# One decode step with gradients on one core: the zero fill reads bf16 instead of u8, the row tiles share one buffer, and the weight gradients are staged in two regions instead of six

## The chip, the core and the metric

The kernel runs on one core of a Trainium2 chip. The number that counts is the device time of one execution in microseconds. The median of three runs of the kernel before is 820.67 us (818.9 to 821.32).

A core has five engines that run side by side: PE (TensorE, matrix products), DVE (VectorE), ACT (ScalarE), POOL (GpSimd) and SP (SyncE). Here SP only issues transfers. Each engine works through its own instructions in order and waits on semaphores for the others. Sixteen DMA engines move data between the main memory of the chip (HBM) and the on-chip buffer (SBUF, 128 partitions). Transfers issued by SP are in one queue, those issued by POOL in another, and both are served by the same sixteen engines.

## The reference

One decode step of a transformer block, forward and backward, for a batch of B = 2, one token, width D = 512.

```python
def _A_ref(x, k_cache, v_cache, wq, wo):      # attention over the last W = 4096 of 32768 cached rows
    q = (x @ wq).reshape(B, Sq, 32, 128).transpose(0, 2, 1, 3)
    k = jnp.repeat(k_cache[:, :, Sk - W:, :], 4, axis=1)      # 8 cached heads, 32 query heads
    v = jnp.repeat(v_cache[:, :, Sk - W:, :], 4, axis=1)
    p = _softmax(jnp.einsum("bhqd,bhkd->bhqk", q, k) * (128 ** -0.5), axis=-1)
    o = jnp.einsum("bhqk,bhkd->bhqd", p, v)
    return o.transpose(0, 2, 1, 3).reshape(B, Sq, 4096) @ wo

def _B_ref(x, w_gate, w_up, w_down):          # F = 1792
    return (_gelu(x @ w_gate) * (x @ w_up)) @ w_down

h = A_x + _A_ref(_layernorm(A_x), A_k_cache, A_v_cache, A_wq, A_wo)
h2 = h + _B_ref(_layernorm(h), B_w_gate, B_w_up, B_w_down)
```

The outputs are `h2` and the gradients, for a given `grad_out`, of A_x, the K cache, the V cache, A_wq, A_wo, B_w_gate, B_w_up and B_w_down, all in bf16. The gradients of the two caches have the caches' own shape (2 x 8 x 32768 x 128): they are zero in all rows but the last 4096 of each head. Those zeros are 224 MiB (32 pieces of 7 MiB) and by far the largest part of what is written.

## The kernel before

**The zero fill.** A tile `zt` of 128 x 1024 zeros is made on DVE by masking a part of w_q with 0 (L118), so it waits for w_q's load. Then POOL issues 32 transfers (`zero_cast`, L104), one for each zero region. Each reads rows of `zt` again and again and casts them to f32 on the way; the bf16 output is seen as f32 for this, so one row of 1024 elements becomes 4 KiB of zeros. In the kernel before `zt` is u8, so a row is 1 KiB at its source. POOL holds eight of these transfers in flight, and issues the next when one has completed.

**The memory.** Nearly all of SBUF is one tile `mem` of 198 KiB in each partition, cut by hand: `at(off, ...)` gives a view at a byte offset, and the tables at the head of the file (`K_OFF`, `PK_OFF`, `OFF_GST`, `OFF_ST` and so on) say which region serves which purpose and when. Order and waits follow from overlaps of these regions; a scheduler in the programming layer puts the instructions of each engine in order when the program is built. Evictions from PSUM to SBUF (`evac`, L88 on DVE and L90 on ACT) take turns between the two engines.

**The stages**, in order of time:

- `attention(0)` and `attention(1)`, one for each batch entry. K and V come head by head through SP (L125, L129). PE turns K (L332), takes the scores (L342), DVE and ACT make the product of K and the exponentials (`pk`, L374 and L377), and PE sums it with V (L382, L388). At batch 1 a later head's K or V goes into a region that an earlier head has left. `pk` of batch 1 is two regions of 4 KiB at 180 and 184 KiB.
- `middle(0)` and `middle(1)`: output projection (L460, L468), second layernorm, feed-forward part and the backward pass down to the gradient of the attention's output. At the end of attention, SP loads w_down again (L137), since K and `pk` have overwritten it, and at batch 1 a copy of the input rows x (L112), which had been overwritten too. L460 is the first matmul of `attn_ps`; it adds x from a tile at partitions 32 and 33 (`x_32`). That tile and `grad_out` (`dh2_bf`, at partitions 0 and 1) are in `dh2_x`, loaded once at the start by ACT (L116, L117) into a pool of their own.
- `score_grads(0)` and `score_grads(1)`: V is turned (L596, copied by L88 and L90) and multiplied by the output's gradient (L605). During `score_grads(1)` the gradients of w_o, w_down, w_gate and w_up are made as well, two units after each step: a unit is one matmul (L665), an eviction into a staging region and, at the end of its group, a store. There are six groups, in this order: 14, 14 and 4 blocks of w_o's gradient (L675), 14 of w_down's (L693), 16 pieces for w_gate and 16 for w_up (L700). Each group has a staging region of its own (`OFF_GST`, L57).
- The gradient of w_q and of x: L225 turns w_q's blocks, L745 makes four blocks of w_q's gradient, each staged in its own 8 KiB of w_q's region and stored by L748. DVE's L726 reads x again here.
- The tail: the last 4096 rows of the caches' gradients. L774 makes them, L88 and L90 evict them into regions of 16 KiB, taken in turn from `OFF_ST` (eight of them), and L782 stores them, 32 transfers of 1 MiB.

Of the kernel before, what the change touches and what calls it, by code (L numbers as in the profile page):

```python
# [16 lines left out]
P = 128  # L17
B, D = 2, 512
HQ, HKV, REP, DH = 32, 8, 4, 128
# [4 lines left out]
NBH = B * HQ  # L24
F = 1792
NFR = F // P
NDR = D // P
# [17 lines left out]
OFF_DS = (196 * KIB, OFF_M)  # L45
MEM_BYTES = 198 * KIB
OFF_R0, OFF_R1, OFF_R2 = OFF_R, OFF_R + 2 * KIB, OFF_R + 4 * KIB
OFF_LN2B, OFF_DHB, OFF_X = OFF_R + 6 * KIB, OFF_R + 7 * KIB, OFF_R + 8 * KIB

K_OFF = ([OFF_WG + (g % 4) * 8 * KIB for g in range(HKV)],  # L50
         [OFF_WD, OFF_WD + 8 * KIB, 32 * KIB, 40 * KIB, 48 * KIB, 56 * KIB, OFF_WD, OFF_WD + 8 * KIB])
# [2 lines left out]
          [OFF_WD + 16 * KIB + i * 4 * KIB for i in range(2)])  # L54

OFF_BD = OFF_WO
OFF_GST = [OFF_WG, OFF_WG + 14 * KIB, OFF_WO, OFF_WO + 14 * KIB, 0, 16 * KIB]  # L57
OFF_FROW = OFF_WD
OFF_DH = OFF_WD + 4 * KIB
OFF_L = OFF_WD + 5 * KIB  # L60
OFF_RO = OFF_WD + 6 * KIB
OFF_ST = [OFF_WG, OFF_WG + 16 * KIB] + [i * 16 * KIB for i in range(4)] + [OFF_WQ, OFF_WQ + 16 * KIB]

@with_exitstack
def kernel(ctx, tc, A_x, A_k_cache, A_v_cache, A_wq, A_wo, B_x, B_w_gate, B_w_up, B_w_down, grad_out,
                out_0, out_1, out_2, out_3, out_4, out_5, out_6, out_7, out_8):
    nc = tc.nc
# [5 lines left out]
    rows = ctx.enter_context(tc.tile_pool(name="rows", bufs=1))  # L73
# [22 lines left out]
    dVv = out_3[:, :, Z:, :].rearrange("b g (p j) d -> p b g j d", p=P)  # L96

    ZE = 1024
    zt = const.tile([P, ZE], U8)
    zero_regions = [o[b, g, 0:Z, :].rearrange("r d -> (r d)") for o in (out_2, out_3) for b in range(B) for g in range(HKV)]  # L100

    def zero_cast(i):
# [1 line left out]
        nc.gpsimd.dma_start(out=zero_regions[i].bitcast(F32).rearrange("(p k e) -> p k e", p=P, k=nper),  # L104
                            in_=zt[:].unsqueeze(1).to_broadcast([P, nper, ZE]))

    dh2_x = rows.tile([34, D], BF16)
    dh2_bf, x_32 = dh2_x[0:B, :], dh2_x[32:32 + B, :]
    x_bf = at(OFF_X, [B, D], BF16, "x")

    def load_x():
        nc.sync.dma_start(out=x_bf[:], in_=A_x.rearrange("b s d -> (b s) d"))  # L112
    load_x()
    wq_sb = at(OFF_WQ, [P, NDR, HQ * DH], BF16, "wq")
    nc.sync.dma_start(out=wq_sb[:], in_=A_wq.rearrange("(p r) n -> p r n", r=NDR))
    nc.scalar.dma_start(out=dh2_bf, in_=grad_out.rearrange("b s d -> (b s) d"))  # L116
    nc.scalar.dma_start(out=x_32, in_=A_x.rearrange("b s d -> (b s) d"))  # L117
    nc.vector.tensor_scalar(out=zt[:].bitcast(U32), in0=wq_sb[:, 0, 0:ZE // 2].bitcast(U32), scalar1=0, scalar2=None,  # L118
                            op0=ALU.bitwise_and)

    Kt, Vt = {}, {}
# [17 lines left out]
    def load_wg_wu():  # L139
# [31 lines left out]
    for base in (0, -HQ):  # L171
        nc.gpsimd.affine_select(out=maskC[:], in_=maskC[:], compare_op=ALU.not_equal, fill=1.0,
                                base=base, pattern=[[-1, HQ]], channel_multiplier=1)
    selB = const.tile([B, NBH], BF16)
    nc.gpsimd.memset(selB[:], 1.0)
    nc.gpsimd.affine_select(out=selB[:], in_=selB[:], compare_op=ALU.is_ge, fill=0.0,
                            base=0, pattern=[[1, NBH]], channel_multiplier=-HQ)
    nc.gpsimd.affine_select(out=selB[:], in_=selB[:], compare_op=ALU.is_ge, fill=0.0,
                            base=HQ - 1, pattern=[[-1, NBH]], channel_multiplier=HQ)
    for i in range(len(zero_regions)):  # L180
        zero_cast(i)

# [10 lines left out]
        nc.vector.tensor_copy(out=y_bf[:], in_=y[:])  # L193
        return mv, rstd

    def transpose_rows(ps, src_bf, name, strided):
        for r in range(NDR):
            src = src_bf[:, r::NDR] if strided else src_bf[:, r * P:(r + 1) * P]
            nc.tensor.transpose(out=ps[:, r, :], in_=src, identity=ident_bf[:B, :B])
# [73 lines left out]
    def prefetch(b, g):  # L273
        if b == 0:
            if g == 0:
                for i in range(4):
                    load_k(0, i)
                    load_v(0, i)
                for i in range(4, HKV):
                    load_v(0, i)  # L280
            elif g + 3 < HKV:
                load_k(0, g + 3)
            if g == 1:
                nc.sync.dma_start(out=wo_sb[:], in_=A_wo.rearrange("(p r) n -> p r n", r=NOR))
        else:
            if g == 0:
                for i in range(4):
                    load_k(1, i)
                    load_v(1, i)
                load_k(1, 4)  # L290
                load_k(1, 5)
            elif g in (1, 2):
                load_k(1, g + 5)
            elif g - 3 + 4 < HKV:
                load_v(1, g + 1)
        if g == HKV:
            if b == 0:
                load_wg_wu()
            load_wd()
            if b == 1:  # L300
                load_x()

    def attention(b):
        with tc.tile_pool(name="ps_KT", bufs=2, space=PSUM) as ps_KT, \
# [135 lines left out]
            nc.vector.tensor_scalar(out=p_bf[b][:], in0=ps[:].rearrange("p a k -> p (a k)"), scalar1=rl[:, 0:1], scalar2=None, op0=ALU.mult)  # L440

    ln2_bf = at(OFF_LN2B, [B, D], BF16, "ln2b")
    dh_bf = at(OFF_DHB, [B, D], BF16, "dhb")
    O2 = small.tile([P, NOR, B], BF16)
    nc.vector.memset(O2[:], 0.0)
    dact = small.tile([P, NFR * B], F32)
# [6 lines left out]
    dh = at(OFF_R2, [B, D], F32, "dh")  # L453

    def middle(b):
        h0 = b * HQ
        with tc.tile_pool(name="ps_W", bufs=2, space=PSUM) as ps_W, \
# [88 lines left out]
            nc.vector.tensor_copy(out=dh_bf[:], in_=dh[:])  # L546
            dhT = transpose_rows(ps_B.tile([P, NDR, B], BF16, tag="sm", name="psT_dh"), dh_bf[:], f"dh{b}", strided=False)

            dO2_ps = ps_B.tile([P, NOR, B], F32, tag="da", name="dO2_ps")

# [70 lines left out]
    score_grads(0)  # L621
    attention(1)
    middle(1)

    o_bhd = small.tile([NBH, DH], BF16, tag="bhd")
    DH_bf = at(OFF_DH, [NBH, D], BF16, "DH")
# [9 lines left out]
    with tc.tile_pool(name="ps_G", bufs=2, space=PSUM) as ps_G:  # L636
# [5 lines left out]
        nc.tensor.matmul(out=DH_ps[:], lhsT=selB[:], rhs=dh_bf[:], start=True, stop=True)  # L642
# [4 lines left out]
        GST = 14 * D  # L647
# [3 lines left out]
        def add_group(n_cols_list, lhsT_fn, rhs_fn, store_fn):  # L651
            st_box = {}
            offs = [0]
            for n in n_cols_list:
                offs.append(offs[-1] + n)

            def unit(k):
                def f():
                    if k == 0:
                        st_box["st"] = at(OFF_GST[gst_i[0]], [P, GST], BF16, "gst")  # L660
                        gst_i[0] += 1
                    st = st_box["st"]
# [48 lines left out]
    with tc.tile_pool(name="ps_W2", bufs=2, space=PSUM) as ps_W, \  # L711
# [19 lines left out]
        nc.vector.tensor_copy(out=dh_bf[:], in_=dx[:])  # L731
        nc.sync.dma_start(out=out_1.rearrange("b s d -> (b s) d"), in_=dh_bf[:])

        L_ps = ps_Q.tile([NBH, D], F32, tag="x")
        nc.tensor.matmul(out=L_ps[:], lhsT=selB[:], rhs=ln2_bf[:], start=True, stop=True)
        L_bf = at(OFF_L, [NBH, D], BF16, "L")
        nc.vector.tensor_copy(out=L_bf[:], in_=L_ps[:])
        gwq_v = out_4.rearrange("(p r) n -> p r n", r=NDR)
        for r in range(NDR):
            st = at(OFF_WQ + r * 8 * KIB, [P, HQ * DH], BF16, "gq")  # L740
            for c4 in range(4):
                ps = ps_G.tile([P, 1024], F32, tag="ps_g", name="ps_gq")
                for q in range(2):
                    col0 = c4 * 1024 + q * 512
                    nc.tensor.matmul(out=ps[:, q * 512:(q + 1) * 512], lhsT=L_bf[:, r::NDR],  # L745
                                     rhs=Ro_flat[:, col0:col0 + 512], start=True, stop=True)
                evac(st[:, c4 * 1024:(c4 + 1) * 1024], ps[:])
            nc.sync.dma_start(out=gwq_v[:, r, :], in_=st[:])  # L748
# [63 lines left out]
```

## Time and profile before

| | |
|---|---|
| median of three runs | 820.67 us |
| the profiled execution | 820.67 us, span 819.0 us |
| mean granted TensorE clock | 0.817 |
| PE, DVE, ACT, POOL busy | 595.0, 510.1, 443.7, 35.9 us |
| DMA | 332.48 MB in 69462 packets, mean 406 GB/s |
| POOL's queue (q0, the zero fill) | 57856 packets, 234.88 MB |
| SP's queue (q1) | 11532 packets, 96.74 MB |
| `prefetch`, L137 at batch 1 | issued at 477.19 us |
| stores of the six weight-gradient groups | issued at 579.4, 590.3, 593.4, 617.9, 640.4 and 657.4 us |
| first store of the tail (L782) | issued at 712.0 us |

The span runs from the first to the last instruction of the profiled execution; the time is that of the whole execution. A line of a timeline has the start and the duration in us, the engine, the line of the kernel, the operation, output and inputs, shapes and count, and in square brackets how long the engine had been idle before and what released it. A line of the DMA view has a queue's packets, its megabytes and the time of its packets as a share of what sixteen engines have in the window; it can be over 100%, since the packets of an engine overlap. "DMA to landing" is the time from a transfer's issue to its semaphore.

### The profile page before, as it was taken

The numbers are of one execution on the slowest core, as the hardware profiler recorded it, in microseconds if no ns is written. First come the engines' busy times: TensorE is split into PE (matmuls) and PEld (weight loads), VectorE is DVE, ScalarE is ACT, GpSimd is POOL, SyncE is SP. The second block draws the span as 40 slices with busy tenths as digits, with TensorE's granted clock in tenths as the row PEclk, the third lists the DMA queues.
The fourth block names the chain that finished last, engine by engine and source line by source line (L and its number), as shares of the span: only waits on it lengthen the run. The fifth ranks groups of instructions, "written<-read, shape, count | busy, mean of one in ns | idle before, by whom it ended". The sixth has DMA issues, their size and how long they took to land.

```text
span 819.0 us, 13345 instructions
## 1 busy us (share of the span) xinstructions
PE 595.0 (73%) x5350; PEld 324.3 (40%) x5350; DVE 510.1 (62%) x893; ACT 443.7 (54%) x1016; POOL 35.9 (4%) x49
## 2 busy tenths in 40 slices
PE   3787877808978845878574786977988697777782
PEld 3454443307566533444242334564433242222220
DVE  2899789703243323979485762435656637999993
ACT  1898889403333423979383742332645434576683
POOL 4100000001000000000000000000000000000000
PEclk9999999965866985989697895955956587888897
DMA  8999999999999999999999999999999999976968
GB/s 363 415 422 418 420 422 422 428 420 424 422 423 422 417 416 425 423 421 419 424 425 422 423 429 418 424 423 423 427 416 423 426 424 425 363 296 281 389 274 343
DMA packets 69462, 332.48 MB, mean 406 GB/s; under 512 B 1804, under 2 KB 1816, under 8 KB 59288
## 3 DMA queue, kind: packets, MB, share of 16 engines
q0 software_dynamic: 57856, 234.88, 86.2%
q1 hardware_dynamic: 11532, 96.74, 49.7%
q8 instruction: 42, 0.69, 0.3%
q10 hardware_dynamic: 12, 0.01, 0.2%
q14 instruction: 20, 0.16, 0.1%
HBM read 49.29 MB, written 282.33 MB: 405 GB/s over the span
## 4 chain that ended last, share of the span: by engine, by line
PE 26%; DVE 13%; DMA 11%; ACT 5%; issue 2%; ACTq 0%; DVEq 0%; SPq 0%
DMA mem<-in_A_v_cache_dram 7%; DVE mem L88 5%; ACT mem L90 4%; PE ps_g L774 4%; PE ps_gr L665 4%; PE ps_tb L225 4%; DMA mem<-in_B_w_down_dram 4%; DVE mem L374 3%; PE M_ps L388 3%; PE VT_ps L596 3%; PE dP_ps L605 2%; DVE mem L685 2%; DVE mem L253 2%; PE ps_gq L745 1%; PE d_ln_ps L722 1%
## 5 line engine op out<-in xcount | busy, mean ns | idle before, releaser
L374 DVE TENSOR_TENSOR mem<-mem,ef 128x1024 bf16<-128x1024 bf16 (+1 forms) x256 | 213.7, 875 | 19.0 <-PE M_ps L388 18.9
L377 ACT ACTIVATE mem<-mem,ef 128x128 bf16<-128x128 bf16 x640 | 200.5, 391 | 24.0 <-PE M_ps L388 21.4
L388 PE MATMUL M_ps<-mem 128*128 128x512 bf16 x512 | 142.4, 399 | 36.5 <-DVE mem L374 31.4
L90 ACT COPY mem<-ps_tb 128x512 bf16<-128x512 bf16 x83 | 48.5, 585 | 126.1 <-PE ps_tb L225 74.4
L225 PE MATMUL ps_tb<-ident_bf,mem 128*128 128x128 bf16 x664 | 82.0, 267 | 26.7 <-DMA mem<-in_B_w_down_dram 18.5
L774 PE MATMUL ps_g<-mem 128*128 128x512 bf16 x256 | 81.8, 421 | 24.4 <-ACT mem L90 20.2
L88 DVE COPY mem<-ps_tb 128x512 bf16<-128x512 bf16 x83 | 35.2, 424 | 95.2 <-PE ps_tb L225 63.6
L90 ACT CAST mem<-ps_g 128x512 bf16<-128x512 f32 x128 | 74.7, 585 | 31.9 <-DVE mem L88 27.2
L88 DVE CAST mem<-ps_g 128x512 bf16<-128x512 f32 x128 | 83.2, 687 | 7.4 <-PE ps_g L774 6.6
L388 PEld LDWEIGHTS <-mem 128*128 128x128 bf16 x512 | 42.9, 100 | 98.5 <-DVE mem L374 55.0
L225 PEld LDWEIGHTS <-mem 128*128 128x128 bf16 x664 | 55.5, 129 | 53.3 <-issue 29.7
L332 PE MATMUL KT_ps<-ident_bf,mem 128*128 128x128 bf16 x512 | 46.5, 242 | 31.4 <-DMA mem<-in_A_k_cache_dram 21.3
L90 ACT COPY mem<-KT_ps 128x1024 bf16<-128x1024 bf16 x32 | 32.1, 1002 | 58.4 <-PE KT_ps L332 58.4
L774 PEld LDWEIGHTS <-mem 128*128 128x128 bf16 x256 | 26.6, 104 | 78.8 <-issue 64.9
L104 POOL DMA_DIRECT2D out_dram<-zt x32 | 33.7, 1142 | 517.4 <-DMA out_dram<-zt 506.2
L332 PEld LDWEIGHTS <-mem 128*128 128x128 bf16 x512 | 36.3, 109 | 43.3 <-DMA mem<-in_A_k_cache_dram 21.9
L90 ACT COPY mem<-VT_ps 128x1024 bf16<-128x1024 bf16 x33 | 34.0, 1031 | 33.9 <-PE VT_ps L596 25.6
L605 PE MATMUL dP_ps<-mem 128*128 128x512 bf16 x128 | 45.1, 437 | 4.5 <-ACT mem L90 4.5
L596 PE MATMUL VT_ps<-ident_bf,mem 128*128 128x128 bf16 x512 | 46.5, 242 | 0.9 <-DVE pkT L572 0.9
L596 PEld LDWEIGHTS <-mem 128*128 128x128 bf16 x512 | 37.4, 109 | 24.7 <-issue 17.2
L88 DVE CAST mem<-ps_gr 128x512 bf16<-128x512 f32 (+1 forms) x40 | 26.7, 671 | 28.9 <-PE ps_gr L665 28.8
L382 PE MATMUL oPK_ps<-mem 128*4 128x128 bf16 x512 | 28.8, 235 | 21.5 <-DMA mem<-in_A_v_cache_dram 21.5
(253 smaller groups left out, 626.6 us busy)
## 6 DMA issues: line engine op xcount, KB each, us to landing
out_dram<-zt POOLq DMA_DIRECT2D x32, 7168.0 KB, 163.2
out_dram<-mem SPq DMA_DIRECT2D x36, 1024.0 KB, 10.4
mem<-in_A_k_cache_dram SPq DMA_DIRECT2D x16, 1024.0 KB, 17.4
mem<-in_A_v_cache_dram SPq DMA_DIRECT2D x16, 1024.0 KB, 29.8
out_dram<-mem SPq DMA_DIRECT2D x5, 1792.0 KB, 24.1
mem<-in_A_wq_dram SPq DMA_DIRECT2D x1, 4096.0 KB, 12.2
mem<-in_A_wo_dram SPq DMA_DIRECT2D x1, 4096.0 KB
mem<-in_B_w_down_dram SPq DMA_DIRECT2D x2, 1792.0 KB, 27.3
```

The lines of the kernel that those rows point to most:

```text
L88: nc.vector.tensor_copy(out=out, in_=in_)
L90: nc.scalar.copy(out=out, in_=in_)
L104: nc.gpsimd.dma_start(out=zero_regions[i].bitcast(F32).rearrange("(p k e) -> p k e", p=P, k=nper), in_=zt[:].unsqueeze(1).to_broadcast([P, ...
L225: nc.tensor.transpose(out=ps[:, a, :], in_=src_block(a), identity=ident_bf[:])
L332: nc.tensor.transpose(out=KT_ps[:, jj, :], in_=Kt[b, g][:, u * 8 + jj, :], identity=ident_bf[:])
L374: nc.vector.tensor_tensor(out=pk[:, 0:n, h0:h1, :], in0=Kb[:, j0:j0 + n, :].unsqueeze(2).to_broadcast(shape), in1=ef[:, j0:j0 + n, h0:h1]. ...
L377: nc.scalar.activation(out=pk[:, jj, i, :], in_=Kb[:, j0 + jj, :], func=ACT.Copy, scale=ef[:, j0 + jj, i:i + 1])
L388: nc.tensor.matmul(out=M_ps[:], lhsT=Vt[b, g][:, j, :], rhs=pk[:, jj, :, :].rearrange("p i d -> p (i d)"), start=(j == 0), stop=(j == NJ - 1))
L596: nc.tensor.transpose(out=VT_ps[:, jj, :], in_=Vt[b, g][:, a * 8 + jj, :], identity=ident_bf[:])
L605: nc.tensor.matmul(out=dP_ps[:, c, :], lhsT=dOpad[:, w0:w0 + P], rhs=VT[:, c * 4:(c + 1) * 4, :].rearrange("d a k -> d (a k)"), start=(i = ...
L665: nc.tensor.matmul(out=ps[:, :n], lhsT=lhsT_fn(k), rhs=rhs_fn(k), start=True, stop=True)
L774: nc.tensor.matmul(out=ps[:, a2, :], lhsT=lhs_bf[:, jp * P:(jp + 1) * P], rhs=rhs_bd[:, ap * 2 + a2, gq * 4:(gq + 1) * 4, :].rearrange("q ...
```

## The change

Three things change together.

- `zt` becomes bf16 (2 KiB in each partition instead of 1), so that the zero fill casts bf16 to f32. The fill's rows are 2 KiB at the source, and still 4 KiB at the destination.
- The pool of the row tile goes. `dh2_x` becomes a view of `mem` at 185 KiB with 66 partitions: `grad_out` at 0 and 1, x at 32 and 33, and `dh_bf` (the gradient rows, until now a region of their own) at 64 and 65. Since `pk` of batch 1 passes over these bytes, `load_rows` loads `grad_out` and x a second time at the end of `attention(1)`, through SP, after w_down. The other copy of x is now loaded after `middle(1)`, in a part of the region that M has left. A matmul that reads `dh_bf` takes its other operand from partitions 64 and 65 too, so `selB` has a copy there.
- The six groups of weight gradients use two regions of 14 KiB in turn, and so do the four blocks of w_q's gradient after them. A region is written again when its store has landed. The tail has six regions instead of eight, and begins with the ones that V has left.

```diff
-OFF_LN2B, OFF_DHB, OFF_X = OFF_R + 6 * KIB, OFF_R + 7 * KIB, OFF_R + 8 * KIB
+OFF_LN2B, OFF_XR = OFF_R + 6 * KIB, OFF_R + 7 * KIB
+OFF_X, OFF_X_AGAIN = OFF_LN2B, OFF_M + 2 * KIB
...
-OFF_GST = [OFF_WG, OFF_WG + 14 * KIB, OFF_WO, OFF_WO + 14 * KIB, 0, 16 * KIB]
+OFF_GST = OFF_WG
...
-OFF_ST = [OFF_WG, OFF_WG + 16 * KIB] + [i * 16 * KIB for i in range(4)] + [OFF_WQ, OFF_WQ + 16 * KIB]
+OFF_ST = [i * 16 * KIB for i in range(4)] + [OFF_WG, OFF_WG + 16 * KIB]
...
-    zt = const.tile([P, ZE], U8)
+    zt = const.tile([P, ZE], BF16)
...
-    dh2_x = rows.tile([34, D], BF16)
-    dh2_bf, x_32 = dh2_x[0:B, :], dh2_x[32:32 + B, :]
-    x_bf = at(OFF_X, [B, D], BF16, "x")
...
+    dh2_x = at(OFF_XR, [66, D], BF16, "xr")
+    dh2_bf, x_32, dh_bf = dh2_x[0:B, :], dh2_x[32:32 + B, :], dh2_x[64:64 + B, :]
+
+    def load_rows(eng):
+        eng.dma_start(out=dh2_bf, in_=grad_out.rearrange("b s d -> (b s) d"))
+        eng.dma_start(out=x_32, in_=A_x.rearrange("b s d -> (b s) d"))
+
+    def load_x(off):
+        x_bf = at(off, [B, D], BF16, "x")
         nc.sync.dma_start(out=x_bf[:], in_=A_x.rearrange("b s d -> (b s) d"))
-    load_x()
+        return x_bf
+    x_bf = load_x(OFF_X)
...
-    nc.scalar.dma_start(out=dh2_bf, in_=grad_out.rearrange("b s d -> (b s) d"))
-    nc.scalar.dma_start(out=x_32, in_=A_x.rearrange("b s d -> (b s) d"))
-    nc.vector.tensor_scalar(out=zt[:].bitcast(U32), in0=wq_sb[:, 0, 0:ZE // 2].bitcast(U32), scalar1=0, scalar2=None,
+    load_rows(nc.scalar)
+    nc.vector.tensor_scalar(out=zt[:].bitcast(U32), in0=wq_sb[:, 0, 0:ZE].bitcast(U32), scalar1=0, scalar2=None,
                             op0=ALU.bitwise_and)
...
-    selB = const.tile([B, NBH], BF16)
+    selB_all = const.tile([66, NBH], BF16)
...
             if b == 1:
-                load_x()
+                load_rows(nc.sync)
...
-    dh_bf = at(OFF_DHB, [B, D], BF16, "dhb")
...
     middle(1)
+    x_bf = load_x(OFF_X_AGAIN)
...
-                        st_box["st"] = at(OFF_GST[gst_i[0]], [P, GST], BF16, "gst")
+                        st_box["st"] = at(OFF_GST + (gst_i[0] % 2) * 14 * KIB, [P, GST], BF16, "gst")
...
-            st = at(OFF_WQ + r * 8 * KIB, [P, HQ * DH], BF16, "gq")
+            st = at(OFF_GST + (r % 2) * 14 * KIB, [P, HQ * DH], BF16, "gq")
```

More of the change, by code (lines that the diff above doesn't have):

```diff
@@ L72 @@
     small = ctx.enter_context(tc.tile_pool(name="small", bufs=1))
-    rows = ctx.enter_context(tc.tile_pool(name="rows", bufs=1))
     mem_pool = ctx.enter_context(tc.tile_pool(name="mem", bufs=1))
@@ L105, in zero_cast @@
                             in_=zt[:].unsqueeze(1).to_broadcast([P, nper, ZE]))
-    dh2_x = rows.tile([34, D], BF16)
-    dh2_bf, x_32 = dh2_x[0:B, :], dh2_x[32:32 + B, :]
-    x_bf = at(OFF_X, [B, D], BF16, "x")
-    def load_x():
+    dh2_x = at(OFF_XR, [66, D], BF16, "xr")
[5 more added lines that the diff above has]
+        x_bf = at(off, [B, D], BF16, "x")
         nc.sync.dma_start(out=x_bf[:], in_=A_x.rearrange("b s d -> (b s) d"))
-    load_x()
+        return x_bf
+    x_bf = load_x(OFF_X)
     wq_sb = at(OFF_WQ, [P, NDR, HQ * DH], BF16, "wq")
     nc.sync.dma_start(out=wq_sb[:], in_=A_wq.rearrange("(p r) n -> p r n", r=NDR))
-    nc.scalar.dma_start(out=dh2_bf, in_=grad_out.rearrange("b s d -> (b s) d"))
-    nc.scalar.dma_start(out=x_32, in_=A_x.rearrange("b s d -> (b s) d"))
-    nc.vector.tensor_scalar(out=zt[:].bitcast(U32), in0=wq_sb[:, 0, 0:ZE // 2].bitcast(U32), scalar1=0, scalar2=None,
+    load_rows(nc.scalar)
+    nc.vector.tensor_scalar(out=zt[:].bitcast(U32), in0=wq_sb[:, 0, 0:ZE].bitcast(U32), scalar1=0, scalar2=None,
                             op0=ALU.bitwise_and)
@@ L173 @@
                                 base=base, pattern=[[-1, HQ]], channel_multiplier=1)
-    selB = const.tile([B, NBH], BF16)
[L175 to L179, printed above, removed]
+    selB_all = const.tile([66, NBH], BF16)
+    nc.gpsimd.memset(selB_all[:], 1.0)
+    selB, selB_64 = selB_all[0:B, :], selB_all[64:64 + B, :]
+    for sel in (selB, selB_64):
+        nc.gpsimd.affine_select(out=sel, in_=sel, compare_op=ALU.is_ge, fill=0.0,
+                                base=0, pattern=[[1, NBH]], channel_multiplier=-HQ)
+        nc.gpsimd.affine_select(out=sel, in_=sel, compare_op=ALU.is_ge, fill=0.0,
+                                base=HQ - 1, pattern=[[-1, NBH]], channel_multiplier=HQ)
     for i in range(len(zero_regions)):
@@ L194, in layernorm, with transpose_rows @@
         return mv, rstd
-    def transpose_rows(ps, src_bf, name, strided):
+    def transpose_rows(ps, src_bf, name, strided, p0=0):
         for r in range(NDR):
             src = src_bf[:, r::NDR] if strided else src_bf[:, r * P:(r + 1) * P]
-            nc.tensor.transpose(out=ps[:, r, :], in_=src, identity=ident_bf[:B, :B])
+            nc.tensor.transpose(out=ps[:, r, :], in_=src, identity=ident_bf[p0:p0 + B, p0:p0 + B])
         dst = small.tile([P, NDR, B], BF16, name=f"T_{name}", tag=f"T_{name[:-1]}")
@@ L545, in middle @@
             ln_bwd(d_ln2_ps[:].rearrange("b a p -> b p a"), ln2[:], rstd2, dh2_bf, f"2{b}", dh, at(OFF_R0, [B, D], F32, "tmp"))
-            nc.vector.tensor_copy(out=dh_bf[:], in_=dh[:])
-            dhT = transpose_rows(ps_B.tile([P, NDR, B], BF16, tag="sm", name="psT_dh"), dh_bf[:], f"dh{b}", strided=False)
+            nc.vector.tensor_copy(out=dh_bf, in_=dh[:])
+            dhT = transpose_rows(ps_B.tile([P, NDR, B], BF16, tag="sm", name="psT_dh"), dh_bf, f"dh{b}", strided=False, p0=64)
             dO2_ps = ps_B.tile([P, NOR, B], F32, tag="da", name="dO2_ps")
@@ L641 @@
         DH_ps = ps_G.tile([NBH, D], F32, tag="g", name="DH_ps")
-        nc.tensor.matmul(out=DH_ps[:], lhsT=selB[:], rhs=dh_bf[:], start=True, stop=True)
+        nc.tensor.matmul(out=DH_ps[:], lhsT=selB_64, rhs=dh_bf, start=True, stop=True)
         nc.vector.tensor_copy(out=DH_bf[:], in_=DH_ps[:])
@@ L730 @@
         ln_bwd(d_ln1_ps[:].rearrange("b a p -> b p a"), ln1[:], rstd1, dh[:], "1", dx, at(OFF_FROW + 2 * KIB, [B, D], F32, "tmp"))
-        nc.vector.tensor_copy(out=dh_bf[:], in_=dx[:])
-        nc.sync.dma_start(out=out_1.rearrange("b s d -> (b s) d"), in_=dh_bf[:])
+        nc.vector.tensor_copy(out=dh_bf, in_=dx[:])
+        nc.sync.dma_start(out=out_1.rearrange("b s d -> (b s) d"), in_=dh_bf)
         L_ps = ps_Q.tile([NBH, D], F32, tag="x")
-        nc.tensor.matmul(out=L_ps[:], lhsT=selB[:], rhs=ln2_bf[:], start=True, stop=True)
+        nc.tensor.matmul(out=L_ps[:], lhsT=selB, rhs=ln2_bf[:], start=True, stop=True)
         L_bf = at(OFF_L, [NBH, D], BF16, "L")
```

## The prediction

> **What bounds the kernel now.** The page's slices come first: the row of the DMA engines is full from the second slice on, at about 424 GB/s, until slice 34 (700 us); after that no engine group is full and the last stage (L774 and its evictions) runs on PE, DVE and ACT.
>
> ```profile
> DMA  8999999999999999999999999999999999976968
> HBM read 49.29 MB, written 282.33 MB: 405 GB/s over the span
> out_dram<-zt POOLq DMA_DIRECT2D x32, 7168.0 KB, 163.2
> ```
>
> The zero fill keeps the engines full, and it does not bound the time by itself: 332.48 MB at 424 GB/s are 784 us of the 819. The time goes to compute that waits for small transfers behind the fill. PE's timeline, read for idle time that a DMA ended (last bracket), shows it:
>
> ```profile
> 184.15 1.04 PE L225 MATMUL ps_tb<-ident_bf,mem 128*128 128x128 bf16 x8 [18.47 <-DMA mem<-in_B_w_down_dram]
> 316.92 0.72 PE L332 MATMUL KT_ps<-ident_bf,mem 128*128 128x128 bf16 x5 [16.55 <-DMA mem<-in_A_k_cache_dram]
> 400.56 0.29 PE L382 MATMUL oPK_ps<-mem 128*4 128x128 bf16 x4 [9.96 <-DMA mem<-in_A_v_cache_dram]
> 447.85 0.29 PE L382 MATMUL oPK_ps<-mem 128*4 128x128 bf16 x4 [9.60 <-DMA mem<-in_A_v_cache_dram]
> 506.57 1.44 PE L541 MATMUL ffn_ps<-mem,actT_bf 128*2 128x512 bf16 x3 [4.83 <-DMA mem<-in_B_w_down_dram]
> ```
>
> With 2.58 at 82 us and 1.94 at 467 us this is 64 us. SP's timeline and the chain of waits give one such transfer whole: 1.8 MB of w_down, issued at 477.19, release PE 29.4 us later.
>
> ```profile
> 477.19 0.33 SPq L137 DMA_DIRECT2D mem<-in_B_w_down_dram  x1
> 481.18 0.25 SPq L112 DMA_DIRECT2D mem<-in_A_x_dram  x1
> 477.19 29.33 DMA mem<-in_B_w_down_dram
> ```
>
> Where do 29 us go? The DMA view in 5 us windows, for 480, 485, 490 and 495 us (packets, MB, packet time as a share of 16 engines; q0 is the fill, q1 is SP's queue):
>
> ```profile
> q0 software_dynamic: 525, 2.11, 128.8%
> ...
> q0 software_dynamic: 331, 1.36, 80.7%
> q1 hardware_dynamic: 61, 0.87, 44.1%
> ...
> q1 hardware_dynamic: 87, 0.96, 243.4%
> q0 software_dynamic: 251, 1.03, 59.8%
> ...
> q0 software_dynamic: 520, 2.12, 128.9%
> ```
>
> No byte of w_down moves for 10 us, all of it moves from 487 to 493, and the small packets that end it (19 in the window 493 to 494, at 829% of 16 engines, so 7 us each) stay open until the semaphore at 506. Stores see the same 10 us: issued at 640.44, first packet at 650.9. With idle engines a first packet follows its issue by about 1 us (0.82 to under 2 at the start). So some 9 us of accepted zero rows stand ahead of any new transfer, and again ahead of its closing semaphore. 525 rows in 5 us on 16 engines are 0.152 us a row: 9 us are 59 rows, 59 KiB read as u8 and 236 KiB written as f32.
>
> **What the queue counts.** If it held 59 rows or 236 KiB of output, an engine's 8 rows of a 14 KiB-row store would enter within 3 to 6 us (they alternate one to one with zero rows), and a store issued 11 us after another would find 5 us of pure zeros behind the first. The two weight-gradient stores issued at 579.44 and 590.26 do not: q1 moves 0.34, 0.34 and 0.24 MB in the windows from 594, 595 and 596 us, no gap.
>
> ```profile
> q1 hardware_dynamic: 24, 0.34, 87.0%
> ...
> q1 hardware_dynamic: 38, 0.34, 104.9%
> ...
> q1 hardware_dynamic: 18, 0.24, 62.4%
> ```
>
> That fits a queue limited in source bytes (60 to 80 KiB), which 112 KiB of store rows overfill. I infer it from one burst and a second like it (w_up and w_down at 149 and 157 us).
>
> **The change part by part**, against the profiled execution: 820.67 us, span 819.0, so 1.67 lie around it; the median of the three runs is the same 820.67.
>
> 1. bf16 zeros. Rows still write 4 KiB, so rows, packets and rate stay. If source bytes limit the queue, 59 KiB hold 29 rows: 4.5 us instead of 9, twice per lone transfer (29.4 to 20.4). If rows limit it, nothing changes. I take the first, as the burst is nearer to it; bounds 0 and 4.5 us at each end. Off the six waits this takes 2 (of 2.58), 7.5 (of 18.47: w_down follows w_up in a burst, so 3 at its start and 4.5 at its end), 7 (of 16.55, also a burst), 9, 9 and 1.9: 36 us until 477. Bounds 0 to 36.
>
> 2. Row tiles in the `mem` buffer. At batch 1 `pk` overwrites them, so SP reloads grad_out and x_32 behind w_down (481.2 and about 481.6 in the old time). L460, the first matmul of `attn_ps`, ran at 482.25 without waiting; now it needs x_32, and in the built order the 32 matmuls of L468 and all that follows stand behind it on PE. (Five transposed blocks are put ahead of it; they filled the layernorm's gaps before, so they bring nothing.) The row load ends its queue behind w_down's rows: w_down's landing plus about 1 us. Bounds: 494 + 3 if its semaphore is quick, 518 if its semaphore queues once more. From the first L468 (483.37) to actT (504.43) are 21.1 us, after which L541 starts.
>  - source bytes: 477.2 - 36 + 20.4 + 1 + 21.1 = 483.7 against 506.57: **-22.9**.
>  - rows: 477.2 + 29.4 + 1 + 21.1 = 528.7: **+22.1**.
>
> The Trainium skill (DMA: Bandwidth & Descriptors, Anatomy of one DMA) fits a DMA as 2 us plus its bytes at 436 GB/s. By that w_down would take 6.2 us and a 2 KiB row load 2; the wait would be nearly free and the sum some 22 us better; the row of this trace, 29.4 us beside a full fill, speaks against using the fit here.
>
> 3. Two staging regions for six groups (L660). Group 2 now waits for group 0's store: issued 579.44, landed 18.2 us later (597.6), while its first eviction was at 590.84 and the engines wait in order, with score_grads' VT copies behind it: +6.8 at the old queue, +2.3 with 9 + 4.5 halved to 13.7. Group 3 waits for group 1's store, which had landed before group 3's 599.44 + 6.8 or nearly: 0 to 2, hidden by two VT units that the order now puts ahead. Groups 4 and 5 come 29 us and more after the stores that they wait for, w_q's first two blocks 40 and 27; the longest such store took 27.9: 0, at most 1 each.
>
> 4. w_q's gradient through the same two regions. Its third block (DVE at 689.17) reuses the first's region, stored at 684.09. That store's rows start 10.2 us after issue, take 3.7, and a store with another behind it closes in 2.4: 16.2 us, against 5.1 available: +11 with the fill running, +6.6 with the shorter queue, 2 to 11 (8) if the fill has just ended. The fourth block then finds its region free.
>
> 5. At nothing: the zero tile's write doubles (293 ns, so at most +0.3 us before the first fill; DVE had waited for w_q); two more POOL selects (0.23 us) lie in POOL's 11.2 us wait for that tile; x's reload waits on SP for L575 (561 us), with the next store at 579 queued behind it and its reader (L726) at 649. If that cover were gone, it would be one lone load, 20 to 29 us. Six tail regions for eight: a region returns after three units of 14 us, and tail stores land within 19.
>
> Sum with the shorter queue: -22.9 + 2.3 + 6.6 = -14, span 805. But then the fill still runs in the tail, and the engines' own floor shows: 20 us at 363 GB/s, 325 MB at 422.5 are 790, and one engine still moved zero rows at 735 when most had ended by 712, 15 to 20 us behind: 805 to 810. I take span 807, time **809**. By the Trainium skill's fabric ceiling (same page, 435 GB/s) the bytes need 764 us; the 424 measured leave 20 us less room, and no wider source row can pass it.
>
> **Rivals.**
> - The queue counts rows (slower). Then 1 is zero: 22.1 + 6.8 + 1 + 8 = +38, 858; 494 + 3 for the row load gives 848, 518 gives 869. For it: nothing in the trace shows a bf16 row. Against it: the gapless burst. Between the ends the sum is linear; it changes sign where an end saves 3.3 us, that is, where bf16 zeros keep more than 5.7 us queued.
> - In between (a byte limit near 80 KiB, 6 to 7 us queued): 18 us off the waits leave +13, 820 to 840.
> - The change doesn't do what it says: reading twice the source slows the fill itself. At 5% (403 GB/s) the floor alone is 840. Against it: reads from SBUF are far below writes.
>
> **How the numbers follow.** Source bytes 0.55 (own range 803 to 816), in between 0.15, rows 0.26, slower fill 0.04. 0.3% is 2.5 us, about what can be told from no change here. Faster is nearly all of the first and a little of the second, 0.54; same 0.05; slower 0.41. The range from 802 to 858 leaves out 0.05 below and 0.15 above (half of the rows case, most of the slower fill).
>
> **What would show it.** Right: a lone load's first packet 5 to 6 us after issue, V waits at L382 under 2 us, w_down to PE in 20 us. Wrong: first packets still 10 us after issue and `attn_ps` starting at 507. In either case `attn_ps` must wait for in_A_x, and DVE or ACT at L88 and L90 for group 0's store.

## The result, and the profile after

The changed kernel takes 831.4 us (median of four runs, 830.67 to 833.47), the kernel before 821.0: a ratio of 1.0135 (95% interval 1.0109 to 1.0161). It is slower by 10 us where 809 was forecast. The profiled execution took 831.67 us with a span of 830.0, so the times below compare with the 820.67 and 819.0 of before.

First the page's rows on the transfers (DMA slices, bytes, and the zero fill's landings):

```profile
DMA  8999999999999999999999999999999999476968
HBM read 49.30 MB, written 282.33 MB: 400 GB/s over the span
out_dram<-zt POOLq DMA_DIRECT2D x32, 7168.0 KB, 163.2
```

The fill runs as it did: same landings, and most of the filled slices at 421 to 424 GB/s, as before. Doubling its source cost it nothing that shows. What differs is where the work stood when it ended. PE's timeline, the idle time that a DMA ended in the last bracket:

```profile
183.74 1.04 PE L231 MATMUL ps_tb<-ident_bf,mem 128*128 128x128 bf16 x8 [16.53 <-DMA mem<-in_B_w_down_dram]
316.36 0.71 PE L338 MATMUL KT_ps<-ident_bf,mem 128*128 128x128 bf16 x5 [18.62 <-DMA mem<-in_A_k_cache_dram]
389.94 0.29 PE L388 MATMUL oPK_ps<-mem 128*4 128x128 bf16 x4 [5.51 <-DMA mem<-in_A_v_cache_dram]
486.98 0.58 PE L465 MATMUL attn_ps<-mem,ident_bf 2*2 2x512 bf16 x1 [18.12 <-DMA mem<-in_A_x_dram]
510.85 1.44 PE L546 MATMUL ffn_ps<-mem,actT_bf 128*2 128x512 bf16 x3 [2.74 <-DVE actT_bf L521]
```

The first two waits, the ones ended by w_down and K, hardly moved (18.47 and 16.55 before). V's waits fell from 21.5 to 14.6 us in sum. And the wait for x_32 is new. SP's issues and the chain of waits show the last one (start, us, what):

```profile
460.71 0.33 SPq L141 DMA_DIRECT2D mem<-in_B_w_down_dram  x1
464.77 0.26 SPq L112 DMA_DIRECT2D mem<-in_A_x_dram  x1
464.77 22.16 DMA mem<-in_A_x_dram
```

A row load of 2 KiB, 22 us. The DMA view says where they go, SP's queue (q1) in the windows 465 to 470, 472 to 473 and 473 to 474 us:

```profile
q1 hardware_dynamic: 78, 1.12, 55.3%
...
q1 hardware_dynamic: 23, 0.05, 1072.9%
...
q1 hardware_dynamic: 4, 0.00, 279.9%
```

The data starts 6.1 us after the issue of w_down instead of 10, and all of it is in by 474. Then come the closing writes, packets of 4 bytes, one for each engine that took part: 16 for w_down and two for each row load. They stay open: the four in the last window 11 us each (279.9% of 16 engines). The reader of x_32 waits for them: `attn_ps` starts at 486.98 us, over 13 us after the last row was in. DVE's timeline shows the waits of the shared staging, ahead of group 2 and of w_q's third and fourth block:

```profile
595.93 0.69 DVE L88 CAST mem<-ps_gr 128x512 bf16<-128x512 f32 x1 [7.06 <-DMA out_dram<-mem]
695.54 1.23 DVE L88 CAST mem<-ps_gq 128x1024 bf16<-128x1024 f32 x1 [5.79 <-DMA out_dram<-mem]
706.68 1.23 DVE L88 CAST mem<-ps_gq 128x1024 bf16<-128x1024 f32 x1 [6.67 <-DMA out_dram<-mem]
```

The ledger of the two profiled executions (us, after less before, each row cumulative):

| event | before | after | difference |
|---|---|---|---|
| w_down of batch 1 issued | 477.19 | 460.71 | -16.5 |
| `attn_ps` starts | 482.25 | 486.98 | +4.7 |
| `ffn_ps` starts (L541, L546) | 506.57 | 510.85 | +4.3 |
| first weight-gradient store | 579.44 | 577.83 | -1.6 |
| first block of w_q stored | 684.09 | 683.58 | -0.5 |
| first tail store | 712.0 | 723.40 | +11.4 |
| span | 819.0 | 830.0 | +11.0 |

So 16.5 us were won, the row load took 21.2 of them and more back, and w_q's staging made the loss.

### The profile page after: what moved, and what is told of

Same layout as the page of the kernel before. It is cut to its first block, busy times and chain, and to the rows that moved or that the text cites. A ratio compares the mean times of both kernels' runs of the same rounds, so it can differ in the third digit from the quotient of the medians.

```text
span 830.0 us, 13381 instructions
## 1 busy us (share of the span) xinstructions
PE 589.6 (71%) x5350; PEld 324.1 (39%) x5350; DVE 508.9 (61%) x893; ACT 442.3 (53%) x1016; POOL 36.5 (4%) x51
## 3 DMA queue, kind: packets, MB, share of 16 engines
q0 software_dynamic: 57856, 234.88, 82.3%
## 4 chain that ended last, share of the span: by engine, by line
PE 25%; DVE 14%; DMA 13%; ACT 5%; issue 2%; ACTq 0%; DVEq 0%; SPq 0%
DMA mem<-in_A_v_cache_dram 6%; ACT mem L90 5%; DVE mem L88 4%; DMA out_dram<-mem 4%; PE ps_g L780 4%; DVE mem L380 4%; PE ps_tb L231 4%; DMA mem<-in_A_x_dram 3%; PE ps_gr L671 2%; PE M_ps L394 2%; PE VT_ps L601 2%; DVE mem L259 2%; PE dP_ps L610 2%; PE d_ln_ps L728 1%; PE attn_ps L473 1%
## 5 line engine op out<-in xcount | busy, mean ns | idle before, releaser
L383 ACT ACTIVATE mem<-mem,ef 128x128 bf16<-128x128 bf16 x640 | 199.5, 391 | 18.6 <-PE M_ps L394 16.5
L394 PE MATMUL M_ps<-mem 128*128 128x512 bf16 x512 | 139.0, 391 | 33.6 <-DVE mem L380 31.7
L231 PE MATMUL ps_tb<-ident_bf,mem 128*128 128x128 bf16 x664 | 81.7, 266 | 23.6 <-DMA mem<-in_B_w_down_dram 16.5
L671 PE MATMUL ps_gr<-mem 2*128 2x512 bf16 (+1 forms) x78 | 31.2, 473 | 18.3 <-DVE mem L88 7.8
```

Source lines behind the costliest of these rows:

```text
L231: nc.tensor.transpose(out=ps[:, a, :], in_=src_block(a), identity=ident_bf[:])
L383: nc.scalar.activation(out=pk[:, jj, i, :], in_=Kb[:, j0 + jj, :], func=ACT.Copy, scale=ef[:, j0 + jj, i:i + 1])
L394: nc.tensor.matmul(out=M_ps[:], lhsT=Vt[b, g][:, j, :], rhs=pk[:, jj, :, :].rearrange("p i d -> p (i d)"), start=(j == 0), stop=(j == NJ - 1))
```

## What a closing write waits for

The prediction took the 12 us between w_down's last byte and its semaphore for the same 9 us of accepted zero rows that stand ahead of its first byte. The first byte now comes 6.0 to 6.1 us after the issue (all lone transfers between 335 and 690 us; 9.9 to 10.6 before), and the closings did not follow: the slowest closing write of each lone V load lasts 12.2, 13.6, 16.2, 15.7 us before and 12.0, 17.1, 14.0, 13.4 us after. Listing the 4-byte packets of the trace one by one gives another reading. After, around w_down and the row loads:

```
SP's queue: 20 closing writes, open from 472.3-473.5; they end at
  472.6 472.7 473.0 473.0 | 480.9 | 482.8 482.9 483.0 483.4 483.5 | 486.5 ... 488.8 (10)
the fill's queue: 16 closing writes of zero DMAs, 0.05 us each, end at
                            480.9 | 482.8 ... 483.5 (5)           | 486.5 ... 488.8 (10)
```

They end together, one with one, to 0.01 us; the trace doesn't name the engines, so that each pair is one engine's is inferred. It is so over the whole of the traces: between 40 us and the fill's last 20 us, 237 of the 271 closing writes of SP's queue that last over 1 us end within 0.02 us of one of the fill's in the kernel before, and 242 of 307 in the changed one. Most of the rest (25 of 34, 44 of 65) end with a row of SP's own queue or within 1.6 us of the first row of SP's next transfer. Theory: **a closing write that has nothing behind it in its own queue on that engine lands only when the zero DMA which the engine is working on closes.** Between 335 and 500 us POOL issues a new zero DMA every 17 to 23 us, as one completes, so the wait is anything from 0 to some 20 us, whatever the source type. The four that ended in 0.2 us can be the ones with row packets behind them on their engines. The rival is the prediction's own backlog. In the experiments below, all edits are against the changed kernel unless they say otherwise.

**Zero DMAs in halves** (changed kernel).

```diff
-    nc.gpsimd.dma_start(out=zero_regions[i]..., in_=zt...to_broadcast([P, nper, ZE]))
+    dst = zero_regions[i]...
+    for k in range(0, nper, nper // 2):
+        nc.gpsimd.dma_start(out=dst[:, k:k + nper // 2, :], in_=zt...to_broadcast([P, nper // 2, ZE]))
```

> The changed kernel with each zero DMA issued as two of half the size (64 of 3.5 MB instead of 32 of 7 MB); rows, bytes and source type stay. Boundary theory: the closing 4-byte write of a load that has nothing behind it in SP's queue lands only together with the closing write of the zero DMA that its engine is working on, so halving that DMA halves the wait. The closings of the lone V loads fall from 12 to 17 us (their slowest) to at most 9, the four V waits (14.6 us) go nearly to zero, w_down at 184 comes up to 10 us earlier, x_32 some 8 us earlier: the whole 800 to 815 us, 806 likeliest. Backlog theory (the prediction's: accepted zero rows stand ahead of the closing write once more): the same rows are queued, closings stay at 12 to 17 us, and the time stays at 831 within 3 us.

Measured: 812.66 us, ratio to before 0.9905 (0.9877 to 0.9932). The slowest closings of the V loads are 8.3, 7.1, 6.3, 8.3 us. The waits view, in sum, times, longest:

```profile
PE KT_ps L339 <- DMA mem<-in_A_k_cache_dram: 12.6, 1, 12.6
PE attn_ps L466 <- DMA mem<-in_A_x_dram: 12.1, 1, 12.1
PE ps_tb L232 <- DMA mem<-in_B_w_down_dram: 7.2, 1, 7.2
```

Every one of them is shorter (18.6, 18.1 and 16.5 in the changed kernel), with rows, bytes and type unchanged. Eight DMAs in flight are half as many bytes now, but the rows queued ahead of a new transfer are not fewer: first packets still come 6.0 to 6.2 us after the issue. The backlog theory expected 831 and falls. w_down of batch 1 is issued at 423 us, 37 us earlier than in the changed kernel, and the first tail store at 675, 48 us earlier; but the kernel ends only 19 us earlier. The transfers now end it: 415 to 425 GB/s until 780 us and beyond, and then, in the DMA view of 780 to 812 us (40 slices of 0.8 us):

```profile
GB/s 440 420 420 451 410 425 440 348 307 287 292 312 266 312 251 246 154 67 46 26 31 20 26 36 20 26 31 20 31 20 26 31 20 31 26 26 5 0 0 0
```

26 GB/s is a sixteenth of 422: for the last 13 us, by this estimate, one DMA engine works alone.

**The same edit on the kernel before.**

> The kernel before with each zero DMA issued as two halves, nothing else. Boundary theory: its closings of 12 to 17 us fall to 9 and less too, the waits for w_down and K (18.5 and 16.6 us) lose some 10 us each and those for V some 5 each, and the time falls from 820 to the floor seen in the first experiment, 808 to 813. Backlog theory: no change, 820 within 3 us.

Measured: 811.69 us, ratio 0.9891 (0.9868 to 0.9913). The V waits fall from 21.5 to 10.9 us, the longest waits for w_down and K only to 14.7 and 12.9: less than expected, since a shorter zero DMA moves its ends, too. The total is as the boundary theory has it.

**Something behind each V load.**

```diff
                 load_v(1, g + 1)
+                nc.sync.dma_start(out=behind[:, g - 3, :], in_=M_sb[0:16, (g - 1) * REP, 0:16])
```

> The changed kernel with a 16-row load of 32 bytes a row issued on SP right behind each of the four lone V loads of batch 1; nobody reads what it brings. Boundary theory: a closing write with something behind it in its own queue lands at once, as the 0.2 us closings in the dense bursts do. So V's 16 closings take 0.2 us instead of 12 to 17, PE's four waits for V (14.6 us) go to zero, attention(1) ends at 447 instead of 461, and x_32, issued that much earlier, meets the zero DMA's end of 464 to 469 instead of 487: 18 to 22 us less, 809 to 814. Backlog theory: the small rows stand behind the zero rows like everything else, closings and time stay as they are, 831.

Measured: 814.6 us, ratio 0.9935 (0.9902 to 0.9968). SP's queue in the windows 392 to 393, 393 to 394 and 394 to 395 us, where the second V load ends:

```profile
q1 hardware_dynamic: 33, 0.23, 70.7%
q1 hardware_dynamic: 42, 0.03, 72.5%
q1 hardware_dynamic: 5, 0.01, 5.7%
```

In the changed kernel such a window (377 to 378) reads

```profile
q1 hardware_dynamic: 18, 0.03, 884.2%
```

so its closings last about 9 us each. With the follower 62 of V's 64 closing writes take 0.35 us, ending with the follower's row on their engine, and the other two 0.04 at most. PE no longer waits for any V. This is the most direct of the tests: the fill is untouched, and a queue of zero rows can't be shortened by adding to the traffic behind it. The x_32 wait (21.7 us) stays; nothing follows x_32.

The same trace sets a limit to the theory. The follower's own closing writes have nothing behind them, with SP's next transfer issued 14 us later or more, and yet 62 of these 64 took 0.01 us and none over 2.2. The follower moves rows of 32 bytes from SBUF to SBUF, and the transfers that were seen to wait read from HBM or write to it. Which difference frees it, no run here takes apart. So it is shown that a V load's closing need not wait for the zero DMA's; that the last closing write of a queue always does is not.

**Does the cast matter?** An f32 zero tile needs none. Two edits of the tile (two source lines in one here):

```diff
-    ZE = 1024                              zt = const.tile([P, ZE], BF16)
+    ZE = 512    # first run                zt = const.tile([P, ZE], F32)
+    ZE = 512    # second run               zt = const.tile([P, ZE], BF16)
```

> The changed kernel with an f32 zero tile of 512 elements: 2 KiB are read and 2 KiB written by each row (the bf16 tile read 2 KiB and wrote 4). If the fill's queue holds some 60 KiB of source: 30 rows at 0.077 us each, a lone transfer's first packet 3 to 4 us after its issue instead of 6. If it holds a number of output bytes (the 5 us of the bf16 fill are some 130 KiB): 6 us again. In both cases the closings stay at 12 to 17 us by the boundary theory, so the time gains little: 824 to 831 if the rate of the fill holds at 423 GB/s.

Measured: 865.15 us, and neither theory had it. SP's queue in the window 339 to 340 us, where a V load ends, and the fill's row of the page:

```profile
q1 hardware_dynamic: 17, 0.06, 14.1%
...
q0 software_dynamic: 57856, 234.88, 71.5%
```

Closings last 0.01 to 0.03 us, the V waits are gone, x_32 releases PE at 416 us and the last tail store is issued at 740; but the page's mean is 385 GB/s, with most slices between 370 and 405, and the kernel ends with the fill, whose last packet ends at 861 us of the span of 863.5. First packets come 4.2 to 5.2 us after issue, between the two expectations. The packets are not what the edit was meant to bring: 57856 as in the changed kernel, of 4 KiB and not of 2.

> The changed kernel with the bf16 zero tile at 512 elements: 1 KiB read, cast, 2 KiB written by each row, so the f32 experiment with the cast put back. If the closings of that experiment were prompt (0.01 us) for want of a cast: here they last up to the zero DMA's end again, 10 us and more. If it was its shorter or twice as many rows: 0.01 us here too.

Measured in a single run: 820.43 us; the slowest closings of the V loads are 12.7, 10.7, 12.7 and 13.5 us again. Here the fill does move rows of 2 KiB, in twice as many packets:

```profile
q0 software_dynamic: 115200, 234.88, 100.8%
```

So rows of 4 and of 2 KiB close late with a cast, and packets of 4 KiB close at once without: the long closings belong to the casting fills, and not to the size or number of their rows. In every casting fill here the source is also smaller than the destination, and the rate higher (most slices at 411 GB/s and more, against 370 to 405); these are not told apart from the cast itself. The Trainium skill (DMA: Bandwidth & Descriptors, Queues, rings and completion order) says that a semaphore increment is a strongly ordered write, which lands only after every earlier write of its DMA engine, across the queues. That a close can wait for another queue's rows agrees with these runs (12 us and more); that a follower in its own queue ends the wait within 0.35 us, that an SBUF-to-SBUF follower doesn't wait at all, and that a fill without a cast causes no wait, does not follow from it.

## What each part of the change is worth

**u8 tile, the rest as changed.**

> The changed kernel with the u8 zero tile of before: the row loads and the staging alone. If the bf16 tile is what brought attention(1) to its end 16.5 us sooner and shortens the first packet's delay from 10 to 6 us: first packets 10 us after issue again, attn_ps at 507, 18 to 26 us more than the changed kernel, 850 to 857. If the tile's type does little and the earlier end came from where the loads meet the ends of the zero DMAs: first packets 10 us, but the time within 8 us of 831.

Measured: 854.3 us, ratio 1.0409 (1.038 to 1.0439), with first packets 10.0 to 10.5 us after issue again and `attn_ps` at 503.9. So the bf16 tile is worth 23 us, and the row loads with the staging cost 34 without it.

**The staging of before, the rest as changed.**

```diff
-OFF_GST = OFF_WG
+OFF_GST = [OFF_WG, OFF_WG + 14 * KIB, OFF_WO, OFF_WO + 14 * KIB, 0, 16 * KIB]
...
```

> The changed kernel with the staging of before: six regions for the weight gradients, four for w_q's, eight for the tail. If the staging costs what the changed trace shows (7.1 us ahead of group 2, 5.8 and 6.7 us ahead of w_q's third and fourth block, with group 2's given back by 640 us): 12 us less, 819. If those waits only stand in for others (the fill's end setting the tail): under 4 us less, 828 to 832.

Measured: 820.68 us, ratio 1.0004 (0.9988 to 1.002): 10.7 us less than the changed kernel, about as the waits have it. The staging is as much as the whole loss, and the tile and the row loads together come out at nothing. That does not make the row loads free: the wait for x_32 is still 17.4 us in this run.

**The row loads ahead of w_down.**

```diff
+            if b == 1:
+                load_rows(nc.sync)
             load_wd()
-            if b == 1:
-                load_rows(nc.sync)
```

> The changed kernel with the two row loads issued ahead of w_down in batch 1 instead of behind it. Boundary theory: the row loads' closing writes now have w_down's rows behind them on their engines and land at once, so attn_ps starts some 7 us after the issue, at 468 instead of 487, w_down's own closing at 489 stays hidden behind 21 us of work, and the whole is 19 us shorter: 812, with 4 us either way for where the later stores meet the zero DMAs' ends. Backlog theory: the closing write stands behind 5 to 13 us of zero rows wherever the load is issued; x_32 would release PE at 474 to 481 and the whole would be 818 to 825.

Measured: 831.29 us, and it tells nothing about either theory, as the order of the loads did not change. SP still issued w_down first (458.55) and grad_out behind it (462.32): the rows wait for the last reader of `pk`, and the scheduler probably put the load that was free earlier in front. The order in the source is not the order in the queue.

**x_32 loaded one group earlier**, into a region that no `pk` overwrites.

```diff
+    x_32b = at(OFF_KT + 3 * KIB, [34, D], BF16, "x32b")[32:32 + B, :]
...
+            elif g + 1 == HKV:
+                nc.sync.dma_start(out=x_32b, in_=A_x.rearrange("b s d -> (b s) d"))
...
-                load_rows(nc.sync)
+                nc.sync.dma_start(out=dh2_bf, in_=grad_out.rearrange("b s d -> (b s) d"))
...
```

> The changed kernel with batch 1's x_32 in a region that is free one group earlier, loaded during the last group and not behind w_down; grad_out stays behind w_down. If the row load's closing is what ate the gain: attn_ps starts at 461 to 462 instead of 487, L546 then waits for w_down's closing at 489 instead of starting at 511, and the whole is 19 to 22 us shorter: 810, from 806 to 816 for where the later stores meet the zero DMAs' ends. If the gain is eaten by the next thing anyway (the stores' closings, the end of the fill): under 6 us less, 825 to 831.

Measured: 814.44 us, ratio 0.9918 (0.9887 to 0.995). PE's timeline:

```profile
465.70 0.37 PE L468 MATMUL attn_ps<-mem,ident_bf 2*2 2x512 bf16 x1 [0.33 <-DVE rl L445]
489.07 1.44 PE L549 MATMUL ffn_ps<-mem,actT_bf 128*2 128x512 bf16 x3 [3.89 <-DMA mem<-in_B_w_down_dram]
```

`attn_ps` starts without a wait for x_32, 4 us later than expected since attention ends at 465, and `ffn_ps` starts at 489.07, on the closing of w_down, as expected; 22 us earlier than in the changed kernel, of which 17 arrive at the end.

**All together**: x_32 early, the staging of before, and zero DMAs in halves or in sevenths.

> The changed kernel with batch 1's x_32 loaded one group early, the staging regions of before, and each zero DMA in two halves. The compute is then ready far ahead of the fill: the first tail store at 650 to 660 instead of 723. If the transfers' own total then ends the kernel (332.5 MB at 422 GB/s are 788 us, behind a slower start, with one DMA engine some 20 us behind the others at the end as in the first experiment): 808 to 812, no better than that one. If compute still shares in the end: 800 to 807.

> The same with each zero DMA in seven parts of 1 MB (224 in all). Boundary theory: a part lasts some 2.5 us, closings of lone loads are 3 us at most and PE waits for none of them. The time is that of the transfers, 805 to 812, if the many small DMAs keep the rate of 422 GB/s; if POOL's issues (1.04 us each) or eight of them in flight are too little for that, the rate falls below 415 and the time is over 815.

Measured: 812.5 us (0.9882, 0.9865 to 0.9898) and 815.7 us (0.9921, 0.9906 to 0.9936). With sevenths no closing of a V load lasts over 2.5 us and PE waits for none; the first tail store goes out at 635 us, 88 us ahead of the changed kernel. Nothing comes of it, as the transfers end the kernel, and with 224 small DMAs the fill loses some GB/s. The kernel before with halved zero DMAs and no other edit (811.69, ratio 0.9891) is as fast as the halved kernel with all of them (ratio 0.9882).

## Why the prediction was wrong

- **What bounds the kernel**: right. The fill alone doesn't, waits for small transfers do, and a floor shows once they go. It was put some us too low, at 805 to 810: the four variants with shorter zero DMAs end between 811 and 816. The lag of one engine, 13 us of it alone, is that floor's last part.
- **Step 1, the start of a lone transfer**: right, 4 us saved of 4.5 forecast; the first packet comes at 6.1 us, where 5 to 6 was to be its sign. Its next sign, V waits under 2 us, did not come: the longest is 5.5.
- **Step 1, "4.5 us at the closing semaphore"**: this is the step that failed. It equated two numbers that were alike by chance, 9 us ahead of the data and some 12 behind it. The saving there is 0.3 us in the mean of the V loads (14.4 to 14.1). The trace of before held the counter-evidence: in its dense bursts the closings last 0.2 us beside the same fill, which a backlog can't explain. What the runs showed in its place is a wait for the closing of the zero DMA in work, or for the next row in the load's own queue, which the source type leaves as it was. Hence -36 us until the end of attention became -16.5: V -6.9 instead of -20, w_down -1.9 instead of -7.5, K +2.1 instead of -7. The holes of step 5 below are 6.0 of the 16.5, and some 5 us of it have no named wait (PE's L388 alone is 3.4 us shorter over the two stages, 142.4 to 139.0; what made it so was not tried).
- **Step 2, the row load**: its mechanism was right (x_32 behind w_down, PE waiting), its closing had the same error: 26.3 us from w_down's issue to `attn_ps` instead of 21.4. Then the work from `attn_ps` to `ffn_ps`, taken over as 21.1 us, lasted 23.9. The 32 matmuls of this stage, before and after:

```profile
483.37 7.07 PE L468 MATMUL attn_ps<-mem,O_164 128*2 128x512 bf16 x32
487.49 9.74 PE L473 MATMUL attn_ps<-mem,O_162 128*2 128x512 bf16 x32
```

  The granted clock is 1.00 from 483.1 to 490.6 us before and 0.72 from 487.4 to 497.3 after, where PE had waited 18 us; with x_32 early and no wait it is 1.00 again, and they take 7.07 us. At `ffn_ps` +4.3 stands for the -22.9 forecast. Of the 27.2 us between them 19.5 are missing from the -36, 4.9 are the row load, and 2.8 are these matmuls and what follows. The Trainium skill (DMA: Bandwidth & Descriptors, Anatomy of one DMA) gives its fit, 2 us and the bytes at 436 GB/s, for a DMA on the gpsimd path; w_down and the row loads are issued by SP, so the prediction stretched it. As an estimate it would give a row load of this size 2 us; 22.2 were measured, and the fit has no term for another queue. With a u8 tile `ffn_ps` starts at 527.0, +20.4. That the rows case had +22.1 is partly luck: `attn_ps` came 3.7 us earlier than its 507.6, and the work behind it took 23.1 us instead of 21.1.
- **Step 3**: group 2 waits 7.1 us instead of 2.3, since group 0's store lands after 18.0 us and not after 13.7. (The 13.7 takes 4.5 off the 18.2 once; halving both 9 and 4.5 would leave 11.4 and no wait.) Of its 16 closing writes six end with zero DMAs, the last at 592.6, and ten with the next store's first rows at about 595. By the first block of w_q all but 1 us is back.
- **Step 4**: the third block waits 5.8 (6.6 forecast), but the fourth does not find its region free: the store issued at 688.24 lands 18.35 us later, and it waits 6.7. The term is 12 instead of 6.6.
- **Step 5, "at nothing"**: no wait shows for what it named (the six tail regions, x's reload), and it left out a gain. In the kernel before PE has five holes of 1.4 to 2.5 us, 10.6 in sum, that the timeline puts down to "issue"; for example:

```profile
350.38 1.67 PE L388 MATMUL M_ps<-mem 128*128 128x512 bf16 x7 [2.54 <-issue]
548.18 0.19 PE L553 MATMUL dO_ps<-T_dh_6165,mem 128*128 128x2 bf16 x2 [2.19 <-issue]
561.23 0.30 PE L575 MATMUL dqM_ps<-dOT_bf,mem 128*128 128x1 bf16 x6 [2.44 <-issue]
```

  In each of the windows 347 to 350, 545 to 548 and 558 to 561 us the instruction queue (q8) moved one packet of 16 KiB. After, there is no such hole over 1 us, and with the u8 tile in the changed kernel there are five again, of 1.2 to 2.4 us. So they belong to the tile. That instruction loads stand behind the fill's rows as data does, and do so for less time now, fits this; no run shows it.
- **The rivals**: the time fell where "in between" put it (820 to 840), but its mechanism, a longer queue, is not what happened: the queue is as short as forecast, so the agreement is luck. "The queue counts rows" is out as a cause, and its sum, 858, is near what the change costs with a u8 tile (854.3).
- **What the queue counts**: three casting fills agree with about 60 KiB of source: with 1 us for an idle start and 0.152 us for a 4 KiB row, 9.2 us are 61 rows of 1 KiB (u8), and 5.1 us are 33 rows of 2 KiB (bf16); the bf16 tile of 512 elements (5.6 to 5.7 us, 0.08 us a row) gives 58 or 59 rows of 1 KiB. These are estimates. The f32 fill, uncast, does not fit (3.2 to 4.2 us at 0.16 us for a 4 KiB packet are 80 to 105 KiB). Open.

## What to carry to other kernels

A small transfer beside a large one has a start and a close, and they have different causes; time each by itself, and test the reading on transfers that have company before halving both. Where a background fill casts, try it in short DMAs (the kernel before went from 821.4 to 811.7 us by this alone), or let something follow each load that is waited for. Before reusing a region or reloading a row, ask which closing semaphore the reuse will wait for: here a 2 KiB reload took 22 us, nearly as long as a 1.8 MB weight.

## What the runs showed of the hardware

- Beside a casting fill, a load from HBM with nothing behind it in its queue mostly closes with the fill's own current DMA: its slowest closing write took 12 to 17 us with zero DMAs of 7 MB, up to 9 with 3.5 MB, up to 2.5 with 1 MB, 0.35 us with a follower in its queue, 0.01 to 0.03 us beside a fill that doesn't cast. A 32-byte SBUF-to-SBUF copy with nothing behind it closed in 0.01 us. Why a cast brings the wait, and why that copy escapes it, is not settled.
- A lone transfer's first packet came 9.9 to 10.6 us after its issue beside the u8 fill, 6.0 to 6.1 us beside the bf16 fill and 4.2 to 5.2 us beside the f32 fill.
- Reading twice the source under a cast left most slices at 421 to 424 GB/s; reading without a cast, as many bytes as are written, brought most of them to 370 to 405.
- The same 32 matmuls took 7.07 us at a granted clock of 1.00, and 9.74 us at 0.72 after PE had waited 18 us. In six other runs with a wait of 12 to 22 us ahead of them they took 8.4 to 9.9 us; without one 7.07 in four runs (the kernel before among them) and 8.40 in a fifth, so the wait is not the whole cause.
- The DMA engines drift apart under a saturating load: at the end of the changed kernel with the halved fill the rate is that of one of 16 for 13 us. What slows it, and which engine it is, was not tried.
